# Small column products in place of full ones at the start of an attention and gated-MLP kernel

## The chip, the cores and the metric

The kernel runs on one core of one Trainium2 chip. The metric is the device time of one execution in microseconds (us). Times of a kernel are given as the median of several runs; one further execution is profiled, and all lines of views come from that one.

## The reference

The input x has 2048 rows of D = 640. It is normalised by row (layer norm without weights), and the result xn feeds two branches whose results are combined.

```
xn = layernorm(x)
# A: attention over 4 segments of 512 rows, 32 heads of 20
q, k, v = xn @ wq, xn @ wk, xn @ wv
for s in range(4):
    a_dot = softmax(causal(q_s k_s^T / sqrt(20))) v_s
    a_mem = (phi(q_s) M) / (phi(q_s) z + 1e-6)      # memory of the earlier segments
    o_s   = sigmoid(beta) * a_mem + (1 - sigmoid(beta)) * a_dot
    M += phi(k_s)^T v_s ;  z += sum(phi(k_s))
s_out = o @ wo
# B: gated MLP with F = 1536
h = sigmoid(xn @ w_gate) * (xn @ w_up)
g = silu(h @ w_down)
out = x + s_out * g
```

## The kernel before

The 2048 rows are four segments of 512 rows, and each segment is four row blocks of 128. Weights stay in SBUF. TensorE carries nearly all of the time: projections to queries, keys and values (tiles psq and psv), gate and up products of the MLP (gp, up), the down product (yp), the scores (Sps), the products of the probabilities with the values (ApsT) and the output product (sp). The order of all instructions on each engine is written out by hand: a list of 80 score units sets slots, a table of times says at which slot a step is placed, and dense products fill what is left between them.

The function `mm` issues a product either as one full 128*128 product (its first call of TensorE, L124) or as four products of 32 output columns of the weights each, one for each quarter of the output partitions (L128). The full form writes all 128 output partitions with one instruction; the column form writes partitions 32r to 32r + 31 with `tile_position=(0, 32 * r)`. The column form is used for the dense products in the slot ahead of an `attend_T` step, whose own products (L565) are in the column form too, as are those of `m_update` (L385).

What matters here is the start, before the first slot:

- x is loaded by row blocks: block 0 in two halves on the SP and ACT queues, block 1 on SP, and so on; halves of wv, then wk and wq follow. The tile `warm` (512 columns of zeros, named mn in the profile) is set by DVE (L149).
- `keep_warm(k)` (L627) issues k full products of 512 columns of zeros by zeros into the PSUM tile `wps`, which nothing reads.
- `keep_warm(9)` is TensorE's first work. It waits for the memset of `warm` alone.
- DVE then takes the statistics of a row block (L637, L639), ACT the root (L642), DVE the reciprocal (L659) and the normalised block xn (L243). For row block 0 `first_transpose` (L650) turns its five 128x128 pieces on TensorE into pT, which ACT (L655) and DVE (L653) copy to xnT. Then one more `keep_warm(1)` follows, and the first half of the values product of block 0 (psv, L124).
- Row blocks 1 to 3 go the same way by `ln_transpose` (L257), with the values products of the blocks before them in between. ACT copies the transposed blocks 1 and 2 (L260) and DVE block 3 (L262); ACT also casts the values (L349).
- After the eight values products come five key products and five query products (psq), then the first gate and up products, and then the slots.

Of the kernel before, what the change touches and what calls it, by code (L numbers as in the profile page):

```python
# [15 lines left out]
L = 512  # L16
# [59 lines left out]
def kernel(  # L76
# [14 lines left out]
    nc = tc.nc  # L91
# [56 lines left out]
    warm = stg.tile([P, 3 * L], BF, name="mn")  # L148
# [98 lines left out]
    def ln_tiles(n):  # L247
        mv = lnp.tile([P, 4, 2], F32, name="mv")
        rs = lnp.tile([P, 4], F32, name="rs")
        return mv, rs  # L250
# [372 lines left out]
    wps = ps_d.tile([P, L], F32, name="wps", tag="d")  # L623

    def keep_warm(k):
        for _ in range(k):
            nc.tensor.matmul(wps[:], lhsT=warm[:, 0:P], rhs=warm[:, 0:L], start=True, stop=True)  # L627

    keep_warm(9)
    mv, rs = ln_tiles(0)  # L630
    new_seg(0)
    xns, sts = {}, {}
# [124 lines left out]
    for p in range(0, OLD, 5):  # L757
        n, g = units[p][0], units[p][1][0][0]
# [214 lines left out]
```

## Time and profile before

| | |
|---|---|
| median of 3 runs | 317.38 us |
| the three runs | 317.27, 318.7, 317.38 us |
| time of the profiled execution | 319.06 us |
| its span, first to last instruction | 317.3 us |
| TensorE (PE) busy | 307.3 us, 97% of the span, 4239 products |
| weight loads (PEld) | 165.8 us, 4268 instructions |
| VectorE (DVE) busy | 224.8 us, 71% |
| ScalarE (ACT) busy | 226.8 us, 71% |
| GpSimd (POOL) busy | 133.9 us, 42% |
| TensorE's instruction loads (queue q8) | 33 of them, 0.54 MB, 0.7% of 16 engines' span |

In a line of a timeline the first number is the start in us from the start of the span, the second the length, then the engine, the line of the kernel, the operation, the tile written and the tile read, the shape, the number of instructions merged, and in brackets the engine's idle time before it and what ended it. For TensorE, 128*32 is the part of the array in use (rows by columns) and 128x512 the moving operand. Products are pipelined: a product's length holds its tail, and the pace is read from the distance of the starts. In a line of the chain the numbers are the start and the length of a step on the path that ended last.

### The profile page before, as it was taken

How to read it: one execution, taken by the hardware profiler on the slowest of the kernel's cores; microseconds unless marked ns; L12 is line 12 of the kernel's file. 1: busy time of each engine (PE TensorE's matmuls, PEld its weight loads, DVE VectorE, ACT ScalarE, POOL GpSimd, SP SyncE). 2: the span in 40 equal slices, each digit the busy share in tenths (PEclk: the TensorE clock that was granted, in tenths of full speed). 3: DMA queues.
4: the chain of work that ended last, by engine and by line, in shares of the span. 5: the costliest groups of instructions: out<-in, count | busy, mean ns of one | idle time of the engine just before them, and what ended most of it. 6: DMA issues, size and time to landing. Idle time of an engine off the chain costs nothing.

```text
span 317.3 us, 10105 instructions
## 1 busy us (share of the span) xinstructions
PE 307.3 (97%) x4239; PEld 165.8 (52%) x4268; DVE 224.8 (71%) x507; ACT 226.8 (71%) x228; POOL 133.9 (42%) x231
## 2 busy tenths in 40 slices
PE   7999999999999999999999999999999999999985
PEld 2544445665445445654665455544466645445663
DVE  5474445665868988888778999788777777634565
ACT  3724477778798776777997869678896766777620
POOL 2870035535263445335443354454443353535312
PEclk9999999999999999999999999999999999999999
DMA  7984885420851362405953385137523001250202
GB/s 251 365 325 148 301 216 164 117 53 2 217 154 58 100 166 106 105 23 160 253 163 97 111 144 146 44 118 214 168 83 119 19 23 44 105 127 0 88 20 83
DMA packets 55245, 41.26 MB, mean 130 GB/s; under 512 B 25952, under 2 KB 53824, under 8 KB 55200
## 3 DMA queue, kind: packets, MB, share of 16 engines
q1 hardware_dynamic: 52656, 35.87, 39.5%
q10 hardware_dynamic: 2544, 4.75, 4.0%
q8 instruction: 33, 0.54, 0.7%
q14 instruction: 12, 0.10, 0.1%
HBM read 19.98 MB, written 14.73 MB: 109 GB/s over the span
## 4 chain that ended last, share of the span: by engine, by line
PE 91%; DMA 3%; DVE 2%; issue 1%; ACT 1%; SPq 0%; ACTq 0%
PE up L124 11%; PE gp L124 10%; PE psq L124 10%; PE yp L124 8%; PE Sps L541 8%; PE gp L128 6%; PE yp L128 6%; PE up L128 6%; PE ApsT L565 5%; PE psv L124 5%; PE psq L128 4%; PE sp L124 3%; PE sp L128 3%; PE psv L128 2%; PE sp L525 1%
## 5 line engine op out<-in xcount | busy, mean ns | idle before, releaser
L549 ACT ACTIVATE pt<-Sps 128x2048 bf16<-128x2048 f32 x80 | 150.3, 1878 | 40.8 <-PE Sps L541 40.0
L551 POOL TENSOR_SCALAR_AFFINE_SELECT pt<-pt 128x512 bf16<-128x512 bf16 x128 | 82.8, 662 | 156.7 <-ACT pt L549 156.7
L432 DVE SCALAR_TENSOR_TENSOR hT<-tg,up 128x512 bf16<-128x512 bf16 x48 | 32.6, 678 | 23.9 <-PE up L124 10.0
L124 PE MATMUL up<-xnT,Wu 128*128 128x512 bf16 x146 | 40.3, 380 | 1.4 <-issue 1.1
L124 PE MATMUL gp<-xnT,Wg 128*128 128x512 bf16 x146 | 38.9, 379 | 0.6 <-issue 0.5
L124 PE MATMUL yp<-Wd,hT 128*128 128x320 bf16 x246 | 38.5, 299 | 0.4 <-issue 0.4
L421 ACT ACTIVATE tg<-gp 128x512 bf16<-128x512 f32 x48 | 28.5, 595 | 14.3 <-PE gp L124 10.0
L541 PE MATMUL Sps<-QT,KT 23*128 23x384 bf16 (+3 forms) x512 | 31.8, 301 | 0.1
L124 PEld LDWEIGHTS <-hT 128*128 128x128 bf16 x246 | 22.7, 98 | 11.9 <-issue 3.6
L573 DVE STREAM_TRANSPOSE tb<-ApsT 128x512 f32<-128x512 f32 x31 | 22.0, 711 | 4.3 <-PE ApsT L565 4.2
L128 PE MATMUL gp<-xnT,Wg 128*32 128x512 bf16 x352 | 24.4, 380 | 0.0
L449 DVE SCALAR_TENSOR_TENSOR aa<-t,yp 128x320 bf16<-128x320 bf16 x32 | 15.3, 477 | 12.4 <-ACT t L448 12.2
L565 PE MATMUL ApsT<-pt,V 128*32 128x512 bf16 (+2 forms) x496 | 23.5, 299 | 0.0
L124 PEld LDWEIGHTS <-Wu 128*128 128x128 bf16 x159 | 14.2, 98 | 17.4 <-issue 4.0
L124 PEld LDWEIGHTS <-Wg 128*128 128x128 bf16 x152 | 14.1, 98 | 15.8 <-issue 1.9
L128 PE MATMUL yp<-Wd,hT 128*32 128x320 bf16 x552 | 21.9, 300 | 0.0
L128 PE MATMUL up<-xnT,Wu 128*32 128x512 bf16 x324 | 21.7, 380 | 0.0
L541 PEld LDWEIGHTS <-KT 23*128 23x128 bf16 x512 | 9.1, 92 | 23.5 <-issue 23.2
L585 DVE STREAM_TRANSPOSE obT<-ob 128x256 f32<-128x256 f32 x31 | 13.5, 434 | 11.1 <-POOL ob L582 11.1
L582 POOL TENSOR_TENSOR ob<-tb,rb 128x320 bf16<-128x320 f32 x27 | 19.9, 737 | 2.3
L124 PE MATMUL psq<-xnT,Wq 128*128 128x512 bf16 x82 | 19.4, 379 | 0.2
L124 PE MATMUL psv<-Wv,xnT 128*128 128x320 bf16 x115 | 18.6, 299 | 0.4 <-ACT xnT L655 0.2
(122 smaller groups left out, 441.0 us busy)
## 6 DMA issues: line engine op xcount, KB each, us to landing
KT<-Kd SPq DMA_DIRECT2D x32, 80.0 KB
QT<-Qd SPq DMA_DIRECT2D x32, 80.0 KB
out_dram<-xt SPq DMA_DIRECT2D x14, 160.0 KB
Wg<-in_B_w_gate_dram ACTq DMA_DIRECT2D x1, 1920.0 KB
Wu<-in_B_w_up_dram ACTq DMA_DIRECT2D x1, 1920.0 KB
xt<-in_A_x_dram SPq DMA_DIRECT2D x3, 640.0 KB
Wd<-in_B_w_down_dram SPq DMA_DIRECT2D x1, 1920.0 KB
Xd<-xn SPq DMA_DIRECT2D x12, 160.0 KB
```

The lines of the kernel that those rows point to most:

```text
L124: nc.tensor.matmul(out_, lhsT=lhsT, rhs=rhs, start=start, stop=stop, skip_group_check=True)
L128: nc.tensor.matmul(out_[cols], lhsT=lhsT[:, cols], rhs=rhs, start=start, stop=stop, tile_position=(0, 32 * r), skip_group_check=True)
L421: nc.scalar.activation(tg[:], gp[:], ACT.Tanh, scale=0.5)
L432: nc.vector.scalar_tensor_tensor(out=h[:], in0=seg[n]["tg"][:], scalar=1.0, in1=up[:], op0=ALU.add, op1=ALU.mult)
L449: nc.vector.scalar_tensor_tensor(out=s["aa"][j][:, hs], in0=t2[:], scalar=1.0, in1=yp[:], op0=ALU.add, op1=ALU.mult)
L541: nc.tensor.matmul(Sps[:, r, c0:c0 + ncol], lhsT=KT[32 * r:32 * r + DH + 3, g, kb * P:(kb + 1) * P], rhs=QT[32 * r:32 * r + DH + 3, g, q0: ...
L549: nc.scalar.activation(pt[:, :, 0:ntot], Sps[:, :, 0:ntot], ACT.Exp, scale=SCALE)
L551: nc.gpsimd.affine_select(out=pt[:, :, c0:c0 + P], in_=pt[:, :, c0:c0 + P], compare_op=ALU.is_ge, fill=0.0, base=0, pattern=[[0, 4], [1, P ...
L565: nc.tensor.matmul(ps[32 * r:32 * r + 32, q0:L], lhsT=Vflat[n % 2][:, off:off + 32], rhs=t[:, r, c0:c0 + ncol], start=(i == 0), stop=(i == ...
L573: nc.vector.transpose(tb[:].rearrange("p h e -> p (h e)"), ps[:].rearrange("p (a t b) -> p a b t", t=32, b=2))
L582: eng.tensor_tensor(to, of, by, op=ALU.mult)
L585: nc.vector.transpose(s["obT", g // 4][:, g % 4, :].bitcast(F32), ob[:].rearrange("p a e b -> p (a e b)").bitcast(F32))
```

## The change

The call `keep_warm(9)` is replaced by `keep_warm_columns(17, L // 2)`. It issues 17 rounds of four products. Each of the four takes 32 columns of the zero weights and 256 columns of the zero moving operand, and writes 32 of the 128 partitions of the same PSUM tile `wps`. The later `keep_warm(1)` stays as it was, and so does the order of everything else.

```diff
@@ -626,7 +626,13 @@
         for _ in range(k):
             nc.tensor.matmul(wps[:], lhsT=warm[:, 0:P], rhs=warm[:, 0:L], start=True, stop=True)
 
-    keep_warm(9)
+    def keep_warm_columns(k, n):
+        for _ in range(k):
+            for r in range(4):
+                nc.tensor.matmul(wps[32 * r:32 * r + 32, 0:n], lhsT=warm[:, 32 * r:32 * r + 32], rhs=warm[:, 0:n],
+                                 start=True, stop=True, tile_position=(0, 32 * r), skip_group_check=True)
+
+    keep_warm_columns(17, L // 2)
     mv, rs = ln_tiles(0)
     new_seg(0)
     xns, sts = {}, {}
```

## The prediction

> **What bounds the kernel now.** I read the page's chain first: it is TensorE's time almost alone, so whatever moves TensorE's dense work by some amount moves the end by as much.
>
> ```profile
> PE 91%; DMA 3%; DVE 2%; issue 1%; ACT 1%; SPq 0%; ACTq 0%
> ```
>
> The change touches only what TensorE does before its first real product, so the second view is the chain over the first 26 us, in order of time (start, length, what). The reader is to see that the products of the change are not on it.
>
> ```profile
> 1.71 4.32 DMA xt<-in_A_x_dram
> ...
> 6.05 0.49 DVE st L637
> ...
> 6.84 0.46 DVE xn L243
> ...
> 7.35 0.47 PE pT L257 x5
> ...
> 7.84 0.70 ACT xnT L260
> ...
> 10.90 2.72 PE psv L124 x20
> 13.62 0.22 PE psq L124
> ```
>
> The chain starts with the load of x, goes through the statistics of the second row block, and only from about 10.7 us on is it TensorE without a break. Third view: TensorE's timeline of the start.
>
> ```profile
> 1.24 3.69 PE L627 MATMUL wps<-mn 128*128 128x512 bf16 x9 [1.24 <-DVE mn L149]
> 5.26 0.45 PE L650 MATMUL pT<-ident,xn 128*128 128x128 bf16 x5 [0.32 <-DVE xn L243]
> 5.55 0.38 PE L627 MATMUL wps<-mn 128*128 128x512 bf16 x1
> 6.17 1.07 PE L124 MATMUL psv<-Wv,xnT 128*128 128x320 bf16 x5 [0.24 <-ACT xnT L655]
> ```
>
> The nine products end at 4.93 and TensorE then idles 0.32 us until xn is there. Fourth, the pace within the nine. The granted-clock column of the stretches reads 1.00 even here, so the pace must be read from the spacing: weight loads of L627, one for each product, at 3.77 and 4.20, and the ninth product on TensorE's timeline at 4.55.
>
> ```profile
> 3.77 0.15 PEld L627 LDWEIGHTS <-mn 128*128 128x128 bf16 x1 [0.28 <-issue]
> 4.20 0.15 PEld L627 LDWEIGHTS <-mn 128*128 128x128 bf16 x1 [0.28 <-issue]
> 4.55 0.38 PE L627 MATMUL wps<-mn 128*128 128x512 bf16 x1
> ```
>
> 0.43 us apart is half the pace of the later 128x512 products (25 psq products from 18.85 on take 5.56 us, less a tail of 0.16: 0.216 each). The step from 4.20 to 4.55 is 0.35 us, between the two; with 0.28 us at the one pace and 0.07 at the other it makes one product (0.28/0.427 + 0.07/0.216 = 1), so full pace came at about 4.20 + 0.28 = 4.48 us, that is 3.24 us after the first product at 1.24. In this execution everything real already ran at full pace.
>
> **The change, part by part.** *Removed:* nine products of 512 columns, 9 x 0.427 = 3.84 us at the half pace they had. *Added:* 17 rounds of four 128*32 products of 256 columns. Do the four of a round run side by side? The trace has the same form at full pace:
>
> ```profile
> 153.63 1.27 PE L128 MATMUL yp<-Wd,hT 128*32 128x320 bf16 x32
> 10.74 2.88 PE L124 MATMUL psv<-Wv,xnT 128*128 128x320 bf16 x20
> 98.19 0.82 PE L385 MATMUL dm<-V,ktok 128*32 128x63 bf16 x80
> ```
>
> Eight rounds of four in 1.27 us, less the last one's tail of about 0.16, are 0.139 us a round; twenty full products in 2.88, less the same tail, are 0.136 each. So a round of four costs what one full product of as many columns costs. The 80 products of 63 columns, weight loads included, take 0.82 - 0.19 = 0.63 us, 8 ns each, so 32 ns for four, 64 at half pace: issuing isn't the limit for rounds of 256 columns. A round is then half of 0.427 = 0.213 us at half pace, and 17 of them 3.63 us. Bounds: 3.63 side by side, and 68 x 0.213 = 14.5 us if one after the other; I take the first, since three groups of column products show it.
>
> So the stream would end at 1.24 + 3.63 = 4.87 at half pace throughout, or, if full pace comes at 4.48 (15.2 rounds done, 1.8 left at 0.108), at 4.67 plus its tail. Both lie ahead of 5.20, when DVE ends xn (start 4.75, 0.45 long). The 0.21 us saved against 3.84 become idle time in front of 5.26: worth nothing. The cover is 5.26 - 4.87 = 0.39 us; a stream longer than about 4.0 us pushes the first transposes. Going over from column products to full ones falls into that idle time too.
>
> *Instructions:* 68 products and 68 weight loads for 9 and 9, 118 more on TensorE. Its code comes in 33 loads of 16 KB (0.54 MB), one per some 258 instructions; each takes 0.7% of 16 x 317.3 us / 33 = 1.1 us of one DMA engine. No wait on them shows in the chain, and the moved loads would fall into the saturated first 20 us. Bounds 0 and 1.1 us; I take 0, as for the 33 loads of now. No other engine's order, no DMA, no wait and no queue (SP's, ACT's, POOL's) is touched: the same zeros, the same accumulator, one wait on the same memset.
>
> *The clock.* This is the only term that can matter, and the trace does not show column products at half pace bringing it up. Bounds: onset at 4.48 as now (cost 0), or the column products count for nothing and the onset is earned by the real work. The price of the late onset, by rows: from 5.26 to 13.46 TensorE has 20 transposes of 0.056, one product of 0.216 and 40 of 0.136, together 6.8 us in 8.2, so 1.4 us of idle time can be eaten, all of it before 10.5. At doubled durations, the 5 transposes end at 5.82, L627's single product at 6.25, the first five psv (after ACT's copy) at 7.7, then transposes 8.2, psv 9.5, psv 10.9, transposes 11.6. With an onset at 5.26 + 3.24 = 8.5 some 0.5 us is left over at 13.46; with an onset at 5.26 + 2 x 3.24 = 11.7, what remains is 25 psv and 5 transposes, 3.4 + 0.28 us, ending at 15.3: +1.8 us. After that TensorE is the chain to the end, so the cost stays. I take 0: four column products side by side fill the same 128x128 array for the same time as a full one, and L128's column products stand in the middle of the run at full pace.
>
> [...]
>
> *Sum:* 0 us from the stream, 0 from the code, 0 from the clock. The profiled execution took 319.06 with a span of 317.3; the sum against it is 319.06 + 0, and I apply the same 0 to the median of 317.38: 317.4 us. The three times lie from 317.27 to 318.7, 0.45% apart, so 0.5% (1.6 us) is about what a measurement can tell from no change.
>
> **The rivals.**
> *Late by one stretch:* full pace only at about 4.48 + 3.24 = 7.7 in the typical execution. By the same working most of the loss before that is idle time eaten, some 0.3 us remain: 317.7. For it: the stream is 0.21 us shorter. [...] Against: TensorE has work up to 4.9 in both. It stays within 0.5%.
> *Slower, column products don't raise the clock:* the onset is earned by real work, at 11.7, +1.8 us, 319.2. It decides from an onset at about 11.3, where the loss reaches 1.6 us; one stretch more (15 us) would cost some 3.3, 320.7. For it: only full 128*128 products precede the onset in this trace, and the real work up to 8.5 has gaps (0.32, 0.24 and more). Against: a round fills the array, and the rows of 128*32 stand at full pace later.
> *Faster:* the unprofiled executions of before may get their clock later than the profiled one (318.7 is 1.4 above the lowest), and denser issue could bring it sooner. If they usually start at half pace up to 7.7, the gain is 0.3 (317.1); if up to 11.3, 1.6 (315.8). For it: the spread. Against: two times of three agree within 0.11, and in the profiled execution there is nothing to gain, since the chain runs over the load of x until 6.05.
> *The change doesn't do what it says:* the four run one after the other at half pace, 14.5 us, first transposes at 15.7, and the dense work 10 us later: 327; or only partly, with every us past 5.3 costing up to one. Against: all three column rows.
>
> **How the numbers follow.** As now: 0.50. Late by one stretch: 0.08. Both within 0.5%: 0.58. No clock from column products: 0.26. One after the other, or partly: 0.04. Together slower 0.30: the unseen term is the only one with a price, and its price just passes the bound, so I keep it high. Faster by more than 0.5%: 0.12, because it needs a late clock in the unprofiled runs of before, which no row shows. The range goes from 315.8 (the whole of the faster case) to 319.5 (the slower case at 11.7 and 0.3 beyond); what is left out is the later onsets, some 0.07, one after the other, 0.04, and 0.05 for a scatter of both ends. The likeliest case's own range is 317.0 to 318.2.
>
> **What would show it.** Right: in the new timeline L627's column products start at 1.24, rounds 0.21 apart and then about 0.11 from some 4.5 on, the last ends before 5.2; the first transposes stand at 5.26 and about 0.056 apart; psq's first product at 13.46; the span at 317.3. Wrong, slower: transposes 0.11 apart at 5.26, psv products 0.27 apart past 8 us, psq's first product at 15 or later. Wrong, one after the other: the first transposes past 5.5. Wrong, faster: a span under 316 with the same first 13.5 us would mean that something I count as untouched has moved.

## The result and the profile after

The change is slower: the median is 320.69 us (10 runs, 319.21 to 323.54) against 317.9 us before (10 runs, 317.27 to 320.48), with a ratio on record of 1.0076 and a 95% interval of 1.0048 to 1.0103 (that ratio is not the quotient of the two medians, which is 1.0088). Of all runs here one execution was in a slower state (323.92 us, the profiled one of the kernel with 86 instructions more below), and it is left out of medians and ratios. The profiled execution took 320.65 us with a span of 318.9 us, 1.6 us more than the span before.

The start is as forecast. TensorE's timeline after the change:

```profile
1.24 3.82 PE L632 MATMUL wps<-mn 128*32 128x256 bf16 x68 [1.24 <-DVE mn L149]
5.31 0.45 PE L656 MATMUL pT<-ident,xn 128*128 128x128 bf16 x5 [0.26 <-DVE xn L243]
13.43 5.56 PE L124 MATMUL psq<-xnT,Wk 128*128 128x512 bf16 x24
```

The 68 products take 3.82 us with their tail, the transposes follow at 5.31 in 0.45 us, so at full pace, and the first psq product stands at 13.43, 0.03 us *ahead* of before. Whatever is lost is lost later. To find where, I paired the 80 exponentials of the scores (L549, one for each score unit) of the two traces in order. Up to 60 us each starts 0.02 us earlier than before; from the one at 70.1 us on they are 1.00 us late, from the one at 129.6 us on 2.67, at 298.3 us 2.69. Two steps, of 1.00 and 1.67 us, make nearly all of it. The chain of after now has what it did not have before, time on DMAs in the middle of the run (start, length, what, 53 to 72 us):

```profile
55.29 3.95 DMA Xd<-xn
...
59.34 0.87 DVE xn L243
...
60.91 1.74 DMA Xd<-xn
...
62.66 6.24 DMA xnT<-Xd
...
68.95 0.39 PE psq L124
```

The store of the first normalised block of the second segment takes 3.95 us. DVE's timeline tells who waits for it: the third xn has only two buffers to go to (`bufs=2`) and must wait until the first block is stored. Before, then after:

```profile
57.39 0.41 DVE L243 TENSOR_SCALAR xn<-xt,mv,rs 128x640 bf16<-128x640 bf16 x1
```

```profile
59.34 0.87 DVE L243 TENSOR_SCALAR xn<-xt,mv,rs 128x640 bf16<-128x640 bf16 x1 [1.89 <-DMA Xd<-xn]
```

Before, the third xn starts at 57.39 without a wait, so its first store, issued at 55.32, took at most 2.07 us. The fourth block, its store and the transposing load xnT<-Xd follow later, and TensorE's psq has to wait 0.8 us for that load. For the whole run, the view of the tile xn lists what DVE waited for (us, times); before has no such line:

```profile
  DMA Xd<-xn: 4.0, 3
```

The three places are the three later segments (55, 123 and 191 us). The waits are 1.89, 1.93 and 0.20 us. At the second place the fourth xn has to wait for the second store, issued at 123.44. DVE before, then DVE after, then the chain of after:

```profile
124.63 0.36 DVE L243 TENSOR_SCALAR xn<-xt,mv,rs 128x640 bf16<-128x640 bf16 x1
```

```profile
127.63 0.54 DVE L243 TENSOR_SCALAR xn<-xt,mv,rs 128x640 bf16<-128x640 bf16 x1 [1.93 <-DMA Xd<-xn]
```

```profile
123.44 4.17 DMA Xd<-xn
...
128.09 0.68 DVE hT L432
...
128.81 0.81 PE up L124 x3
```

The next gated product hT, queued behind xn on DVE, comes so late that TensorE's next up product waits 1.5 us for it.

Why are the stores late? The DMA view of 55 to 60 us in 40 slices, before and after:

```profile
GB/s 0 0 0 0 0 0 0 0 0 143 369 389 348 62 0 205 399 389 287 31 0 0 0 0 0 0 66 0 0 174 358 420 307 51 205 389 410 287 21 0
```

```profile
GB/s 0 0 0 0 0 0 0 0 0 326 379 369 256 31 10 276 358 399 174 10 0 0 10 10 76 0 10 10 20 21 31 20 21 0 0 0 0 0 0 0
q8 instruction: 1, 0.02, 2.1%
```

Both show the two stores as two bursts up to about 57.5 us. After the change, a trickle of 10 to 31 GB/s goes on until 59.1 (the 76 within it holds the start of an 8 KB instruction load of another queue, q14). In the trace the trickle is the last 16 of the 256 data packets of the two stores, one sixteenth; they run one after the other, from 57.85 to 59.12. Each store ends with sixteen packets of 4 bytes: 30 of the 32 have come by 57.45, the other two at 58.69 and 59.11. I read this as the share of one DMA engine of the 16; the trace does not name the engine of a packet. And in this stretch the after kernel has a load of TensorE's code (q8, 16 KB in one packet, from 56.19 to 57.87), the before kernel none: its loads stand at 54.10 and 60.92, on either side of the stores. One sixteenth of the stores stood still beside the 16 KB packet and went on at 57.85, as that packet ended (57.87). At the second place the share stands still before the load begins by its record: fifteen sixteenths of the second store move from 124.27 to 124.85, the load is recorded from 125.41 to 126.37, and the missing sixteenth starts at 126.35. There the share stood still for some 2.1 us beside a load recorded with 0.96 us; the runs do not show why.

The step from 2.69 us at the last exponential to 1.6 us in span is in the tail, and most of it is two waits. Before, TensorE waited 0.60 and 0.28 us near 306 us behind a store of OTd of 3.45 us, after there is no such wait. Before had a code load at 301.83 inside that store; whether it was the reason there too was not tried.

### The profile page after: what moved, and what is told of

Read it like the earlier page. It is cut to its first block, busy times and chain, and to the rows that moved or that the text cites. A ratio compares the mean times of both kernels' runs of the same rounds, so it can differ in the third digit from the quotient of the medians.

```text
span 318.9 us, 10222 instructions
## 1 busy us (share of the span) xinstructions
PE 307.7 (96%) x4297; PEld 167.5 (53%) x4327; DVE 225.5 (71%) x507; ACT 226.7 (71%) x228; POOL 134.3 (42%) x231
## 4 chain that ended last, share of the span: by engine, by line
PE 86%; DMA 7%; DVE 3%; issue 1%; ACT 1%; POOL 1%; SPq 0%; DVEq 0%; ACTq 0%
PE up L124 10%; PE psq L124 10%; PE gp L124 9%; PE yp L124 9%; PE Sps L541 8%; PE gp L128 6%; PE up L128 5%; PE ApsT L565 5%; PE psv L124 5%; PE yp L128 4%; PE psq L128 4%; DMA Xd<-xn 4%; PE sp L124 3%; PE psv L128 2%; DMA xnT<-Xd 2%; PE sp L128 2%
## 5 line engine op out<-in xcount | busy, mean ns | idle before, releaser
L549 ACT ACTIVATE pt<-Sps 128x2048 bf16<-128x2048 f32 x80 | 150.2, 1878 | 41.1 <-PE Sps L541 40.3
```

The source lines that it names most:

```text
L549: nc.scalar.activation(pt[:, :, 0:ntot], Sps[:, :, 0:ntot], ACT.Exp, scale=SCALE)
```

## Experiments

**Theory ("code loads").** The 118 added instructions shift every later 16 KB code load to an earlier place in the program; three of them come to lie on the stores of xn, take one DMA engine each (for 1.0 to 1.7 us by their records; that it is one engine is my reading of the sixteenth that came late), and DVE, with two buffers for xn, stands behind the stores. **Rival ("column form").** The column products leave something behind. **Rival ("each instruction").** Every added instruction costs.

**As many instructions without columns.**

```diff
-    keep_warm_columns(17, L // 2)
+    keep_warm_small(68, L // 8)   # full 128*128 products of 64 columns
```

> Sixty-eight full 128*128 products of 64 columns in place of nine of 512: as many instructions as the change (118 more than before) and the same 3.63 us of stream at half pace, but no column form. Theory 'code loads': the 16 KB loads of TensorE's code come 118 instructions earlier in the program, run beside the stores Xd<-xn near 55 to 59, 122 to 127 and 190 us, and DVE waits for those stores (4.0 us in 3 waits with the change, none before); so this kernel is as slow as the change, 320.7 us within 1, with the same three waits. Rival 'column form' (something that column products leave behind): 317.9 as before, no wait of DVE for Xd<-xn.

Measured: 320.1 us, ratio 1.0064 (1.0045 to 1.0083). Code loads at 56.15, 124.44 and 190.68 us, and on the tile xn:

```profile
  DMA Xd<-xn: 3.8, 2
```

Two waits instead of three, but the time is within the 1 us that was expected and the two main losses lie where those of the change do (the exponentials are 0.90 us late at 70, 2.57 at 129.6). The column form is not the cause.

**One load's worth of instructions more.** Before has 33 loads for 8507 recorded instructions of TensorE, one for 258; so 254 more should move each load by about one place.

```diff
-    keep_warm_columns(17, L // 2)
+    keep_warm_columns(34, L // 4)
```

> Thirty-four rounds of four column products of 128 columns: 272 instructions, 254 more than before, the same 3.63 us of stream. [...] Theory 'code loads': 317.9 us within 1, loads near 54 and 61 us again, no wait of DVE for Xd<-xn. Rival 'column form': 320.7 or more. Rival 'each added instruction costs': twice the loss, 323 or so.

Measured: 318.23 us, ratio 1.0011 (0.9991 to 1.0032). Code loads at 55.02, 60.72, 120.56 and 193.93 us (before has 54.10, 60.92, 120.63 and 193.50), no wait of DVE for Xd<-xn, every exponential up to 165 us within 0.03 us of before. Over twice the added instructions cost nothing that is clear of noise: here the place of the loads counts, not the number.

**Half the shift.**

```diff
-    keep_warm_columns(17, L // 2)
+    keep_warm_columns(9, L)
```

> Nine rounds of four column products of 512 columns: 72 instructions, 54 more than before, a stream of 3.84 us as before. Theory 'code loads': the load that stood at 61 us comes at about 58, beside the third and fourth store of xn and no longer the first, the one at 131 stays behind the stores, the one at 193.5 comes at about 190 beside the first store of xn of the last segment: at most one of the three waits, 318 to 319.5. Rival 'column form': 320.7.

Measured: 318.81 us, ratio 1.0039 (1.0015 to 1.0063). Loads at 57.4, 127.99 and 190.27; one wait of DVE for Xd<-xn of 0.7 us, at 192 us in the last segment. Time and wait are as the theory has them, but not all of the loss: of the 1.0 us that the exponentials of this execution lose against before, 0.6 comes at that wait and 0.4 near 168 us, where nobody waits for a store of xn.

**The change with four places for xn.** From the second segment on the four blocks go to the key tile of the segment before, whose last use is over by then.

```diff
-        xn = lnp.tile([P, D], BF, name="xn", bufs=2)
+        if n == 0:
+            xn = lnp.tile([P, D], BF, name="xn", bufs=2)
+        else:
+            xn = seg[n - 1]["kt"][:].rearrange("p c n -> p (c n)")[:, j * D:(j + 1) * D]
```

> The change, but from the second segment on the four normalised blocks xn go to four places of their own (the key tile of the segment before, dead by then) instead of two buffers in turn, so that DVE's third and fourth xn need not wait for the stores of the first and second. Code loads stand as with the change. Theory 'code loads hold up the stores, and DVE stands behind them': DVE's 4.0 us of waits go, TensorE's stalls near 68 and 124 us mostly go, and 317.0 to 318.2 us. Rival 'the loads hold up TensorE itself' or 'column form': the waits of DVE go and the time stays at 320.7.

Measured: 318.0 us, ratio 0.9993 (0.997 to 1.0015). The code loads stand where the change put them, less the time that is no longer lost (56.47, 123.68, 188.52); the trickle is there too, but nobody waits. The third normalised block (now named ktd) on DVE's timeline, and the chain where it ran over Xd<-xn and xnT<-Xd in after:

```profile
57.56 0.41 DVE L246 TENSOR_SCALAR ktd<-xt,mv,rs 128x640 bf16<-128x640 bf16 x1
```

```profile
59.95 3.09 PE yp L124 x22
...
63.37 3.10 PE yp L128 x88
...
68.27 1.08 PE psq L124 x5
```

TensorE never stops there. So the loads do not hold up TensorE itself here; the cost is DVE's wait behind the stores.

**Before with four places for xn.** The same edit on the kernel before.

> The kernel before with four places for the normalised blocks from the second segment on, as in the run with the change; code loads where they stood before. Theory 'code loads hold up the stores, DVE stands behind them': before has no wait of DVE for Xd<-xn in its profile, so little is there to gain: 317.4 to 318.2 us, the same as the change with four places (318.0). Rival 'the four places are a gain of their own, which only hid the cost of the column form': about 2.7 us under before, 315.3.

Measured: 317.99 us, ratio 1.001 (0.9988 to 1.0031). The four places are no gain of their own; they take away what the change had cost and no more.

**Both remedies.** `keep_warm_columns(34, L // 4)` and the four places.

> Both remedies: 34 rounds of 128 columns, which put the code loads back where they were, and four places for xn. Theory: neither has anything left to take from the other: 317.4 to 318.2 us, no wait of DVE for Xd<-xn. If the two add up (under 317.2), each removes something else.

Measured: 318.53 us, ratio 1.0019 (0.9999 to 1.0039), no wait for Xd<-xn. The median is 0.3 us over the range that was expected; they do not add up, and no version here beats the kernel before.

**Other shifts.** `keep_warm_columns(26, 168)` has 190 instructions more than before, `keep_warm_columns(22, 198)` 158, `keep_warm_columns(13, 336)` 86.

> Twenty-six rounds of four column products of 168 columns: 208 instructions, 190 more than before, a stream of 3.64 us. Theory 'code loads': they come 66 instructions later than before, counted from the load ahead: near 55, 122 and 187 us, at the beginning of the stores of xn in the first two places and just ahead of them in the third: one or two waits of DVE for Xd<-xn, 318.5 to 320.5 us, between the 254 (318.2) and the 118 (320.7). Rival 'the more instructions the better past 118' or 'column products as such': no order that follows the loads.

> Twenty-two rounds of four column products of 198 columns: 176 instructions, 158 more than before, a stream of 3.63 us. By the profiles so far the code load near the first stores of xn (at 55.3 and 56.0) came at 56.19 with 118 instructions more and at 54.89 with 190 more, the second at 125.4 and 122.2, the third at 191.1 and 187.6. So here about 55.5, 123.3 and 188.8, each within the first pair of stores. Theory 'one of the 16 DMA engines is taken by the load while it has its share of the store still to move': DVE waits for Xd<-xn in two or three places, 319.5 to 321.0 us. Rival 'more instructions are better past 118' (from 320.7 to 318.2): 319.3 or less.

> Thirteen rounds of four column products of 336 columns: 104 instructions, 86 more than before, a stream of 3.64 us. Between the 54 (loads at 57.4, 128.0, 190.3) and the 118 (56.2, 125.4, 191.1): about 56.8, 126.8 and 190 here. The first load meets the end of the first pair of stores, which is done by 57.4 where nothing is in its way, the second comes after the pair of 121.7, the third within the pair. Theory: one or two waits of DVE, 318.8 to 320.2 us. Rival 'column form': 320.7.

No run shows the 66 instructions of the first of these as such; by the 258 recorded ones for each load of before it would be 68, and with 254 more the loads that are read stand within 1 us of places of before.

All shifts together, columns unless said otherwise, each ratio against the runs of before on the same chip (the three load times are those nearest to the three groups of stores, which begin near 55, 122 and 188 us in before):

| instructions more | median us | ratio and interval | loads near the stores, us | DVE's waits for Xd<-xn |
|---|---|---|---|---|
| 0 (before) | 317.9 | 1 | 54.10, 120.63, 185.86 | none |
| 54 | 318.81 | 1.0039 (1.0015 to 1.0063) | 57.40, 127.99, 190.27 | 0.7 us, 1 |
| 86 | 319.9 (nine executions) | 1.0074 (1.0035 to 1.0113) | not read | not read |
| 118 (the change) | 320.69 | 1.0076 (1.0048 to 1.0103) | 56.19, 125.41, 191.14 | 4.0 us, 3 |
| 118, full form | 320.1 | 1.0064 (1.0045 to 1.0083) | 56.15, 124.44, 190.68 | 3.8 us, 2 |
| 158 | 319.31 | 1.0045 (1.0026 to 1.0064) | 56.00, 123.16, 189.09 | 2.8 us, 2 |
| 190 | 318.24 | 1.0024 (1.0008 to 1.004) | 54.89, 122.18, 187.58 | 0.4 us, 1 |
| 254 | 318.23 | 1.0011 (0.9991 to 1.0032) | 55.02, 120.56, 186.61 | none |

Before's own median is 318.0 us on the chip of the rows with 54, 118 in full form and 254, 317.91 on that of 86 and 158, 317.51 on that of 190. The time rises and falls again within these 254 instructions, and with it DVE's waits. With 190 the median is 0.3 us under the expected range: its load at 54.89 ends at 55.82, just as the packets of the first store begin, and no wait follows there; the one wait is at the second place. It is still 0.7 us over before on its chip, with an interval clear of 1; the profiled execution does not show where. With 158 the median is 0.2 us under the expected range and at the bound that was given to the rival, so the time alone does not decide there; the two waits of 2.8 us do, and so does the change with four places, which keeps the 118 instructions and loses nothing. With 86 the median lies in the expected range; its profiled execution took 4.0 us more than that, so no loads or waits are read from it.

Differences well under 1 us are not all the stores'. Near 168 us the exponentials of the profiled executions also shift, without any wait for xn, from 0.5 us earlier (no first products) to 0.8 later (before with four places). What does that was not tried.

**The clock by itself.** Before with four places for xn, which keeps the stores out of the question, and without the nine first products.

```diff
-    keep_warm(9)
```

> The kernel before with four places for xn and without the nine first products (the one product after the first transposes stays). It prices the clock by itself, free of the waits for the stores: 18 instructions fewer move the code loads little. By the working of the prediction an onset near 8.5 us costs 0.4 to 0.5 us and one near 11.7 costs 1.8, against the kernel before with four places. If the clock were what the change had lost, this kernel would have to lose at least as much: 2.7 us. Theory 'code loads': 0.3 to 1.8 us.

Measured: 319.21 us, ratio 1.0051 (1.0027 to 1.0075), against 317.99 with the nine products: 1.2 us. TensorE's timeline shows half pace in the first transposes (five in 0.71 us) and the full one at 10.05 (five in 0.44 us):

```profile
5.29 0.71 PE L652 MATMUL pT<-ident,xn 128*128 128x128 bf16 x5 [5.29 <-DVE xn L246]
10.05 0.44 PE L260 MATMUL pT<-ident,xn 128*128 128x128 bf16 x5
14.05 1.24 PE L124 MATMUL psq<-xnT,Wk 128*128 128x512 bf16 x4
```

The first psq product comes at 14.05 against 13.46 before, 0.59 us late, with the onset recorded at 9.18 us. Taking the stream away altogether costs less than the change did, and the change's own trace has full pace before its first transposes, so a lost clock was not its cause. This profiled execution took 318.05 us, 1.2 less than the median, and of the 0.59 us only 0.1 is left at the last exponential; so it does not show where the slower executions lose their 1.2 us, and that stays open.

## Why the prediction was wrong

- **The stream:** right. It ends before xn is there, side by side and at 0.213 us a round as worked out (of the three rows that were to show this, the psv one is the full form; the trace of the change now shows it at half pace); no exponential up to 60 us is late.
- **The clock:** right to be taken at 0. Column products brought full pace here as full ones do: with the change the onset is recorded at 5.05 us, ahead of the first transposes at 5.31, so nothing but column products had run. The onset comes 3.81 us after the first product with the change and 3.96 to 4.85 in the seven other runs of the column form, against 3.23, 5.22 and 5.44 in three of the full form. What sets the moment within this scatter of 2.2 us the runs do not show. The onsets up to 6.7 us cost at most 0.35 us (the first exponential of before with four places, onset 6.68), much as the rival "late by one stretch" had it with 0.3, and the price of an onset near 9 us, 0.59, fits the 0.5 worked out for 8.5.
- **The instructions:** this step failed: the term for the code, taken at 0, measured 2.8 us in the median. The prediction had the right numbers (118 more, 33 loads of 16 KB, 1.1 us of one DMA engine each) and then asked only whether TensorE waits for its code. It looked at the loads that move within the first 20 us, while every later one moves as well, and at TensorE as the only one that could suffer. The bound of 1.1 us for all was wrong too: beside a load of 1.0 to 1.7 us a store took some 2 us more, with DVE behind it, and TensorE lost 1.00 and 1.67 us in two places. With four places for xn the same loads cost nothing (318.0 us), which shows that the wait was the price.
- **"No other wait is touched":** wrong in the same way. The program's order and waits are the same, but the DMA engines carry the code as well (queue q8, 0.7% of 16 engines' span before, 0.8% after), and that timing had changed. The profile before had what was needed: the time of each code load, the two buffers of xn, and stores that lay from 55.3 to 59.8 us, just between the loads at 54.10 and 60.92.
- **The rivals:** "column products don't raise the clock" had the right sign and over half of the size (319.2), but by luck, not by its cause: the clock came up, the psq products started on time, and the full form lost nearly as much. The range ended at 319.5, below the 320.69 measured, since it held no case for the code.

## What to carry to other kernels

In this kernel, instructions that cost nothing where they stood moved every later code load of their engine (with the change, the one at 60.92 us to 56.19). So after such an edit, find out where the loads fall, and what small transfer with a waiting engine they meet. A loss by moved code loads can be told from a loss by the edit itself in one run: pad the stream by one load's worth of instructions (258 recorded ones here; 254 did it) and see whether the loss goes. Two buffers between a vector step and its store were enough here only while the store was on time (at most 2.07 us, against 3.95); where a dead tile lent places, in four kernels here, no wait for these stores was left.

## What the runs showed of the hardware that was not expected

- Beside one 16 KB code load (1.68 us in one packet) one sixteenth of two stores of 160 KB came late (16 of 256 packets, by my reading the share of one of the 16 DMA engines), and with it the completion of the whole store: 3.95 us against at most 2.07 without the load there. At the second place the share stood still about 2.1 us (124.27 to 126.35), though the load's record has 0.96.
- The loss follows the place of the load: 54 to 158 instructions lost 0.8 to 2.8 us in the median against before on the same chip, 190 lost 0.7, 254 lost 0.2, within its interval.
- Sixty-eight full products of 64 columns ran at 0.053 us each at half pace, with a weight load each (3.81 us with the tail); this is an eighth of the 0.427 us of a 512-column product at half pace, so neither the small size nor the weight loads slowed them.
